# Rows of two units per batch by transposing DMAs in batches 4 to 7, and a new order of all steps, in an attention and routing kernel

## The chip, the cores and the metric

The kernel runs on one core of a Trainium2 chip. The metric is the device time of one execution in microseconds (us). The core's engines are TensorE (PE, its weight loads PEld), VectorE (DVE), ScalarE (ACT), GpSimd (POOL) and SyncE (SP); each runs its own list of instructions in order and waits on semaphores of the others.

## The reference

Eight batches of 448 tokens. First an attention without a softmax, for 12 heads of 64 columns:

```python
scores = scale * np.matmul(q, k.transpose(0, 1, 3, 2))
attn = np.maximum(scores, 0.0) ** 2 / S
x = np.matmul(attn, v)          # then (batch, token, 768)
```

Then in every batch the 128 tokens with the highest gate score get an expert's output added:

```python
scores = np.einsum('bsd,d->bs', x, w_gate)
top_idx = np.argpartition(-scores[b], capacity)[:capacity]
h = np.maximum(x[b, top_idx] @ w1, 0.0)        # 768 to 1024
ye = h @ w2                                     # 1024 to 768
out[b, top_idx] = x[b, top_idx] + g[:, None] * ye   # g = sigmoid(score); all other rows of out are x
```

## The kernel before

A batch is three units of four heads, so units 0 to 23 are the attention, unit u belonging to batch u // 3. The whole program is one list of steps, the text `ORDER`, written by a planner and emitted item by item: an engine runs its own instructions in the order in which they stand there. Moving an item in the list therefore changes what stands in front of it on its engine, and nothing else. Letters A and D in an item say whether ACT or DVE does the copy out of PSUM.

A unit goes through these steps (u the unit, c one of seven chunks of tokens):

- `L,q,u`, `L,k,u`, `L,v,u`: POOL issues the load of q, k or v (fp32 in DRAM, bf16 in SBUF; six buffers of each). For the units in `BYDMA` the heads are laid out in another way, and the load is issued as two halves of 64 partitions (line 115 and not line 111).
- `T` and `TE`: PE turns q and k, DVE copies them to `qkt`.
- `S,u,c`: PE makes the scores of a chunk (line 260) in two of the eight PSUM banks; `R,u,c`: ACT takes the ReLU of them into `r_sb` (line 216). There are 168 of these ReLUs. A later `S` that uses the same banks waits for the ReLU that empties them.
- `Q,u,c0,c1`: DVE squares `r_sb` into `a_sb`, in two pieces per unit; `V,u,c`: PE multiplies with v (line 281, 28 matmuls per unit).
- `X,u`: ACT or DVE copies the unit's output, token columns along the free axis, to `xT_sb`.
- The rows of the output, token by token, are made in one of two ways. `RT,u` has PE turn `xT_sb` back into PSUM (line 295) and `RE,u` copies it to `x_rows`; or `XB,u` has SP issue two transposing DMAs (line 320) from `xT_sb` to `x_rows`. Before, `XB` is used for all units of batches 5 and 6.
- `ST,b`: POOL issues the store of batch b's rows to `out` (two DMAs).

Each batch b is then routed: `colx`, `colE`, `bt`, `rk`, `cs`, `rank`, `hots`, `sel`, `sE` find the 128 token numbers `idx`; `XG,b` is an indirect gather on POOL (line 443) that reads the rows back from `out`, and so waits for `idx` and for the landing of `ST,b`; `XT` turns them on PE and `xeE` copies them; `gs` and `sig` give the gate; `h,b,f` are the first expert matmuls (line 483, eight steps), `hE` their ReLU into `hT`; `y,b,f` the second ones (line 499), `yE` the copy with the gate into `gye`; `ADD,b` is an indirect accumulating DMA on POOL into `out` (line 517). Batch 7 is not gathered: `xe,7` picks its rows from `x_rows` by matmuls (line 435), with `g,7` (line 353) for its scores, and its `ADD` goes in two halves.

So POOL's queue holds, in one order, the loads, stores, gathers and additions: what stands behind a store that waits for its rows is issued after it.

Of the kernel before, what the change touches and what calls it, by code (L numbers as in the profile page):

```python
# [21 lines left out]
def kernel(  # L22
# [314 lines left out]
    class Moe:  # L337
# [11 lines left out]

        def g(self, i, bank=None):  # L350
            if i == 0:
                self.at["g"] = bank
            nc.tensor.matmul(out=PS[:, self.at["g"], :S],
                             lhsT=wg_col[:, 1, i:i + 1].to_broadcast([128, 128]), rhs=self.xT[:, i].rearrange("p c n -> p (c n)")[:, :S],
                             start=(i == 0), stop=(i == NM - 1), skip_group_check=True)
# [189 lines left out]
    Q,5,0,3 cs0,0,4 cs,0,0 cs,0,1 V,4,0,6 L,v,7 cs,0,2 R,6,0,A V,4,1 V,4,2 S,6,1,0 V,4,3 V,4,4 S,6,2,2 V,4,5
    V,4,6 rank,0 hots,0 Q,5,3,7 R,6,1,A R,6,2,A T,8,0,4 ST,0 T,8,1 TE,8,2,D V,5,0,0 S,6,3,2 V,5,1 X,4,A S,6,4,6
    Q,6,0,3 V,5,2 V,5,3 V,5,4 V,5,5 R,6,3,A S,6,5,2 R,6,4,A R,6,5,A S,6,6,4 V,5,6 RT,4,0,6 R,6,6,A sel,0,7 sE,0
    T,9,0,2 L,k,9 T,9,1 X,5,A RE,4,D S,7,0,4 S,7,1,6 R,7,0,A Q,6,3,7 R,7,1,A colx,1,0,0 colx,1,1 colx,1,2
    S,8,0,4 RT,5,0,1 colE,1 S,7,2,6 bt,1,0 R,8,0,A W,0,4,6 TE,9,2,D S,8,1,2 S,8,2,4 RE,5,D rk,1,0 rk,1,2 L,k,10
    R,7,2,A W,1,6,8 L,q,10 RT,3,0,1 rk,1,1 W,0,2,6 S,7,3,6 R,8,1,A RE,3,D rk,1,3 R,8,2,A Q,7,0,3 V,6,0,2 V,6,1  # L550
    V,6,2 W,0,3,6 L,k,11 R,7,3,A V,6,3 V,6,4 S,7,4,4 R,7,4,A S,7,5,0 T,10,0,6 T,10,1 XG,0 S,7,6,4 TE,10,2,D
    V,6,5 R,7,5,A R,7,6,A V,6,6 X,6,A cs0,1,0 cs,1,0 cs,1,1 cs,1,2 rank,1 hots,1 W,1,2,8 XT,0,0,1 S,8,3,4
    S,8,4,6 R,8,3,A R,8,4,A xeE,0,2,D sel,1,0 sE,1 S,8,5,2 W,0,1,6 h,0,0,0 h,0,1 h,0,2 R,8,5,A S,8,6,4 S,9,0,6
    h,0,3 h,0,4 Q,7,3,7 h,0,5 S,9,1,2 h,0,6 Q,8,0,3 h,0,7 R,8,6,A S,9,2,4 R,9,0,A Q,8,3,7 V,7,0,6 V,7,1 L,v,8
# [10 lines left out]
    L,q,13 T,13,0,0 L,k,13 T,13,1 RE,8,D S,12,3,6 R,11,6,A RE,7,D V,10,0,4 V,10,1 V,10,2 L,q,15 V,10,3 TE,13,2,D
    L,v,12 L,k,17 L,v,14 S,12,4,2 V,10,4 V,10,5 R,12,3,A R,12,4,A S,12,5,0 Q,11,3,7 S,12,6,6 R,12,5,A R,12,6,A
    V,10,6 X,10,A hots,2 T,14,0,2 L,v,15 T,14,1 TE,14,2,D y,1,0,2,0 y,1,1,2 y,1,2,2 Q,12,3,7 L,k,15 S,13,0,6
    S,13,1,2 S,13,2,4 R,13,0,A L,v,13 R,13,1,A L,q,17 y,1,3,2 y,1,4,2 y,1,5,2 sel,2,6 L,k,19 R,13,2,A ST,2
    y,1,6,2 y,1,7,2 sE,2 S,13,3,2 V,11,0,6 R,13,3,A V,11,1 V,11,2 L,q,18 S,13,4,4 V,11,3 V,11,4 R,13,4,A
# [5 lines left out]
    TE,16,2,D cs,3,0 cs,3,1 cs,3,2 rank,3 XG,2 RE,10,A XT,2,0,1 xeE,2,2,D R,14,6,A Q,14,3,7 S,15,0,4 R,15,0,A
    S,15,1,6 S,15,2,2 R,15,1,A h,2,0,0 h,2,1 Q,14,0,3 h,2,2 R,15,2,A h,2,3 L,v,18 S,15,3,4 R,15,3,A S,15,4,6
    h,2,4 h,2,5 h,2,6 h,2,7 hE,2,2,D S,15,5,2 L,q,20 hots,3 V,14,0,4 V,14,1 L,v,17 R,15,4,A V,14,2 S,15,6,6
    L,k,22 V,14,3 V,14,4 V,14,5 V,14,6 Q,15,0,3 R,15,5,A R,15,6,A X,14,A L,q,21 S,16,0,0 S,16,1,2 R,16,0,A ST,3
# [92 lines left out]
```

## Time and profile before

| what | us |
|---|---|
| median of 3 runs | 200.74 (198.83 to 202.49) |
| the profiled execution | 199.68 |
| its span, first to last instruction | 197.9 |
| PE, DVE, ACT, POOL busy in the span | 179.1, 164.7, 162.5, 109.2 |
| mean granted share of PE's clock | 0.987 |

The profiled execution took 1.78 us more than its span, and 1.06 us less than the median. A matmul's busy time includes its passage through the array, so a busy PE may still be one that takes in little. The span has four parts: a start until the first ReLU, a long stretch in which ACT, DVE and PE all work nearly without a pause, a last stretch after the last ReLU in which PE works off the experts of batches 5 to 7, and the last additions.

### The profile page before, as it was taken

To read this page: it belongs to the slowest core of one execution; us is meant where nothing else is said; L and a number is where in the kernel's file an instruction comes from. 1 tells how busy PE (TensorE), PEld (TensorE's weight loads), DVE (VectorE), ACT (ScalarE), POOL (GpSimd) and SP (SyncE) were. 2 spreads that over 40 slices of the span, in tenths; PEclk is the share of its full clock that TensorE was granted. 3 is DMA by queue.
4 is the path that set the end of the run, shared out by engine and by line. 5 is a ranking of instruction groups with operands and counts; after the bars stand their busy time and mean duration, and the time that the engine had idled before them with its cause. 6 is when DMAs were issued, how large, how long until landed. Compare 5 with 4: busy or idle time off the path is not lost.

```text
span 197.9 us, 7244 instructions
## 1 busy us (share of the span) xinstructions
PE 179.1 (91%) x3186; PEld 124.1 (63%) x3186; DVE 164.7 (83%) x234; ACT 162.5 (82%) x204; POOL 109.2 (55%) x160
## 2 busy tenths in 40 slices
PE   7778898989899999999998999999999999999900
PEld 7455455657567675875776767776676466688600
DVE  2489999999989999999999899999997999753310
ACT  4689999999999998999998999899998997242300
POOL 7968654641863967758897694460203140853360
PEclk9999999999999999999999999999999999999995
...
GB/s 175 140 184 203 203 205 205 235 322 206 201 248 298 203 182 200 202 195 283 177 152 172 344 205 288 262 145 170 226 106 106 92 311 55 18 251 240 55 135 24
DMA packets 32333, 37.70 MB, mean 191 GB/s; under 512 B 8744, under 2 KB 29614, under 8 KB 31278
## 3 DMA queue, kind: packets, MB, share of 16 engines
...
## 4 chain that ended last, share of the span: by engine, by line
PE 56%; ACT 17%; DMA 11%; POOL 7%; issue 4%; DVE 2%; POOLq 0%; DVEq 0%
ACT r_sb L216 15%; PE ps L260 12%; PE ps L483 10%; PE ps L499 9%; PE ps L281 7%; PE ps L233 5%; DMA q_sb<-in_q_dram 4%; DMA v_sb<-in_v_dram 4%; PE ps L295 4%; POOL out_dram L517 3%; DMA xg<-out_dram,idx 3%; PE ps L209 2%; PE ps L374 2%; PE ps L362 2%; POOL k_sb L111 1%
## 5 line engine op out<-in xcount | busy, mean ns | idle before, releaser
L216 ACT ACTIVATE r_sb<-ps 128x896 bf16<-128x896 f32 x168 | 140.8, 955 | 8.1 <-PE ps L260 7.1
L274 DVE TENSOR_TENSOR a_sb<-r_sb 128x2688 bf16<-128x2688 bf16 (+1 forms) x48 | 84.9, 1785 | 2.4 <-ACT r_sb L216 2.0
L260 PE MATMUL ps<-qkt 64*64 64x448 bf16 x672 | 55.6, 362 | 4.3 <-ACT r_sb L216 2.5
L281 PE MATMUL ps<-a_sb,v_sb 64*64 64x448 bf16 x672 | 42.1, 351 | 0.8 <-ACT r_sb L216 0.8
L260 PEld LDWEIGHTS <-qkt 64*64 64x64 bf16 x672 | 21.4, 104 | 21.7 <-issue 11.4
L220 DVE COPY qkt<-ps 128x1792 bf16<-128x1792 bf16 (+3 forms) x26 | 26.1, 1006 | 4.4 <-PE ps L233 2.8
L281 PEld LDWEIGHTS <-v_sb 64*64 64x64 bf16 x672 | 21.5, 106 | 9.5 <-issue 2.2
L443 POOL DMA_INDIRECT xg<-out_dram,idx x7 | 12.2, 1748 | 27.4 <-DVE idx L427 23.6
L499 PE MATMUL ps<-w_sb,hT 128*128 128x384 bf16 x128 | 25.2, 326 | 0.0
L483 PE MATMUL ps<-xeT,w_sb 128*128 128x128 bf16 x384 | 24.5, 219 | 0.2 <-DVE xeT L220 0.2
L483 PEld LDWEIGHTS <-w_sb 128*128 128x128 bf16 x384 | 21.8, 98 | 4.5 <-issue 4.2
L517 POOL DMA_INDIRECT out_dram<-gye,idx x9 | 15.7, 1741 | 9.5 <-ACT g__3725 L476 5.9
L216 ACT ACTIVATE xT_sb<-ps 128x896 bf16<-128x896 f32 x16 | 15.4, 963 | 3.0 <-PE ps L281 2.9
L111 POOL DMA_DIRECT2D v_sb<-in_v_dram x18 | 13.2, 731 | 6.5 <-PE ps L281 2.8
L327 POOL DMA_DIRECT2D out_dram<-x_rows x8 | 4.5, 567 | 21.9 <-DMA x_rows<-xT_sb 13.6
L233 PEld LDWEIGHTS <-q_sb 128*64 128x64 bf16 x336 | 11.2, 111 | 6.5 <-issue 5.5
L233 PE MATMUL ps<-ident,q_sb 128*64 128x128 bf16 x336 | 14.1, 223 | 1.1 <-ACT r_sb L216 0.6
L499 PEld LDWEIGHTS <-hT 128*128 128x128 bf16 x128 | 10.6, 97 | 7.2 <-issue 2.2
L111 POOL DMA_DIRECT2D q_sb<-in_q_dram x17 | 12.7, 749 | 4.0 <-PE ps L233 1.5
L111 POOL DMA_DIRECT2D k_sb<-in_k_dram x17 | 12.5, 736 | 3.5 <-PE ps L260 1.5
L233 PE MATMUL ps<-ident,k_sb 128*64 128x128 bf16 x336 | 13.9, 220 | 0.0
L385 DVE SCALAR_TENSOR_TENSOR mask_sb<-ps,cols,tie 128x448 bf16<-128x448 f32 (+2 forms) x24 | 12.3, 546 | 0.7 <-PE ps L374 0.6
(123 smaller groups left out, 196.7 us busy)
## 6 DMA issues: line engine op xcount, KB each, us to landing
...
```

Of the source, the lines that this page charges most:

```text
L111: nc.gpsimd.dma_start(out=dst, in_=src(t, u))
L216: nc.scalar.activation(out=out_, in_=in_, func=func or AF.Copy, scale=scale)
L220: nc.vector.tensor_copy(out=out_, in_=in_)
L233: nc.tensor.matmul(out=PSB[HALF[j], at["T", u, w], n * 128:(n + 1) * 128], lhsT=s[:, j, c, :], rhs=ident, is_transpose=True, start=(n == 0 ...
L260: nc.tensor.matmul(out=PS[HALF[hf], bank + j, :S], lhsT=qkt[u][HALF[j], 1, c, hf, :], rhs=qkt[u][HALF[j], 0, :, hf, :], start=True, stop=True)
L274: nc.vector.tensor_tensor(out=a_sb[u][:, c0:c1], in0=r, in1=r, op=ALU.mult)
L281: nc.tensor.matmul(out=PS[HALF[j], at["V", u] + hf, :S], lhsT=v_sb[u % NBUF][HALF[hf], j, c, :], rhs=a_sb[u][HALF[hf], c, j, :], start=(c ...
L385: nc.vector.scalar_tensor_tensor(out=mask, in0=row[:, o:S], scalar=self.cols[:, c:c + 1], in1=tie[:, :S - o], op0=ALU.subtract, op1=ALU.is ...
L443: read = reads[self.b] = nc.gpsimd.indirect_dma_start(out=self.xg, out_offset=None, in_=out[0:self.b + 1].rearrange("b s d -> (b s) d"), i ...
L483: nc.tensor.matmul(out=PS[:, self.at["h"] + bk, o:o + 128], lhsT=w1_sb[:, m, f * 128:(f + 1) * 128], rhs=self.xeT[:, m, :], start=(m == 0) ...
L499: nc.tensor.matmul(out=PS[:, self.at["y"] + w, :384], lhsT=self.hT[:, f, :], rhs=w2_sb[:, f, w * 384:(w + 1) * 384], start=(f == 0), stop= ...
L517: add = nc.gpsimd.indirect_dma_start(out=out[0:self.b + 1].rearrange("b s (w d) -> (b s w) d", w=w), out_offset=bass.IndirectOffsetOnAxis( ...
```

## The change

`BYDMA` now holds units and not batches: the first two units of each of the batches 4, 5, 6 and 7 (12, 13, 15, 16, 18, 19, 21 and 22) take the transposing DMAs, eight units in place of six; the third unit of each of these batches goes over PE. The gate's column for such a unit is looked up unit by unit (`order`). `h` and `y` get an argument `by64` that splits a matmul's 128 output rows into two halves of 64; it is 0 for all of `h` and 1 for eight steps of `y`, `y,1,4` to `y,1,7` and `y,2,4` to `y,2,7`. The list `ORDER` is a new one throughout: its planner now charges transfers for later loads that overtake them.

```diff
-    BYDMA = (5,6)
+    BYDMA = (12,13,15,16,18,19,21,22)
...
-        if b not in BYDMA:
+        if u not in BYDMA:
             nc.gpsimd.dma_start(out=dst, in_=src(t, u))
             return
...
+        def order(self, m):
+            return 1 - (NU * self.b + m // 2 in BYDMA)
...
-                                     rhs=wg_col[:, 1 - (self.b in BYDMA), m:m + 1],
+                                     rhs=wg_col[:, self.order(m), m:m + 1],
...
-        def y(self, f, part, bank=None):
+        def y(self, f, part, by64, bank=None):
...
-                nc.tensor.matmul(out=PS[:, self.at["y"] + w, :384], lhsT=self.hT[:, f, :],
-                                 rhs=w2_sb[:, f, w * 384:(w + 1) * 384], start=(f == 0),
-                                 stop=(f == NF - 1), skip_group_check=True)
+                for p in HALF if by64 else (slice(0, 128),):
+                    nc.tensor.matmul(out=PS[p, self.at["y"] + w, :384], lhsT=self.hT[:, f, p],
+                                     rhs=w2_sb[:, f, w * 384:(w + 1) * 384], start=(f == 0),
+                                     stop=(f == NF - 1), skip_group_check=True)
...
-    hE,5,2,D V,22,0,4 V,22,1 V,22,2 V,22,3 V,22,4 V,22,5 V,22,6 R,23,5,A R,23,6,A sel,6,0 y,5,0,2,6 y,5,1,2
+    V,22,0,4 V,22,1 V,22,2 V,22,3 V,22,4 V,22,5 V,22,6 R,23,4,A R,23,5,A S,23,6,0 R,23,6,A y,5,0,2,0,2 y,5,1,2,0
```

On ACT, at the end of the attention, there stood (`r_sb_3457` and `r_sb_3589` are the ReLUs of units 22 and 23, `xT_sb1` batch 7's output, `g` a gate):

```order
L476 ACTIVATE g__2525<-ps_84 128x1
L216 ACTIVATE r_sb_3457<-ps_84 128x896 x6
L216 ACTIVATE r_sb_3589<-ps_84 128x896 x7
L216 ACTIVATE xT_sb1_104<-ps_84 128x2x448 x2
L476 ACTIVATE g__2994<-ps_84 128x1
```

And now (`r_sb_3424` and `r_sb_3626` are units 22 and 23, `gye_3612` belongs to batch 4, `hT_3673` to batch 5):

```order
L216 ACTIVATE r_sb_3424<-ps_84 128x896 x6
L216 ACTIVATE gye_3612<-ps_84,g__2541 128x768
L216 ACTIVATE r_sb_3626<-ps_84 128x896 x3
L216 ACTIVATE hT_3673<-ps_84 128x1024
L216 ACTIVATE r_sb_3626<-ps_84 128x896 x4
L216 ACTIVATE xT_sb1_104<-ps_84 128x2x448 x2
```

Two copies that DVE did before, batch 4's `gye` and batch 5's `hT`, now stand between ACT's last ReLUs.

On POOL, in the last third of the program, there stood (`v_sb5` takes unit 23's values, `v_sb4` unit 22's, `x_rows_3076` and `x_rows_3439` are batches 5 and 6, `xg` a gather, `gye` an addition):

```order
L443 DMA xg_3087<-out_0_dram,idx_2524 128x768
L111 DMA v_sb5_102<-in_v_dram 128x2x448
L327 DMA out_0_dram<-x_rows_3076 64x3072
L328 DMA out_0_dram<-x_rows_3076 64x2304
L443 DMA xg_3451<-out_0_dram,idx_2993 128x768
L111 DMA v_sb4_101<-in_v_dram 128x2x448
L327 DMA out_0_dram<-x_rows_3439 64x3072
L328 DMA out_0_dram<-x_rows_3439 64x2304
L517 DMA out_0_dram<-gye_3115,idx_2130 1792x768
```

And now (`x_rows_3283` is batch 6, `v_sb3` and `v_sb5` take the values of units 21 and 23, `gye_2103` and `gye_3169` belong to batches 1 and 3):

```order
L446 DMA xg_3428<-out_0_dram,idx_3019 128x768
L335 MEMSET gap_116 1x1
L523 DMA out_0_dram<-gye_2103,idx_1078 896x768
L115 DMA v_sb3_100<-in_v_dram 64x2x448 x2
L327 DMA out_0_dram<-x_rows_3283 64x3072
L328 DMA out_0_dram<-x_rows_3283 64x2304
L523 DMA out_0_dram<-gye_3169,idx_2189 1792x768
L111 DMA v_sb5_102<-in_v_dram 128x2x448
L446 DMA xg_3773<-out_0_dram,idx_3502 128x768
```

The values of unit 23, the last load of all, moved from in front of batch 5's store to behind batch 6's store and batch 3's addition.

On DVE, at the end of the attention, there stood (`a_sb` are the squares of units 22 and 23, `idx_3384` batch 6's token numbers, `x_rows_3765` the rows of units 22 and 21):

```order
L222 TENSOR_SCALAR xT_sb1_104<-ps_84 128x2x448
L409 TENSOR_TENSOR hot__3383<-slots_127,rank__3382 128x512
L218 TENSOR_SCALAR hT_3676<-ps_84 128x1024
L274 TENSOR_TENSOR a_sb_3716<-r_sb_3589 128x2688
L427 TENSOR_REDUCE idx_3384<-ps_84 128x1
L274 TENSOR_TENSOR a_sb_3716<-r_sb_3589 128x3584
L220 COPY x_rows_3765<-ps_84 128x4x256 x2
L368 TENSOR_TENSOR cols_3720<-ps_84,skew_106 128x4
```

And now:

```order
L430 TENSOR_REDUCE idx_3502<-ps_84 128x1
L274 TENSOR_TENSOR a_sb_3635<-r_sb_3424 128x2688
L222 TENSOR_SCALAR xT_sb1_104<-ps_84 128x2x448
L274 TENSOR_TENSOR a_sb_3786<-r_sb_3626 128x2688
L274 TENSOR_TENSOR a_sb_3786<-r_sb_3626 128x3584
L371 TENSOR_TENSOR cols_3763<-ps_84,skew_106 128x4
```

Batch 6's token numbers moved ahead of unit 22's second square, and the two copies of rows behind the last square are gone.

## Rows read from the trace of the kernel before

**Rows 1.** Busy time by stretch: us, then PE, PEld, DVE, ACT, POOL busy (instructions)

```profile
7.20:160.90 153.70, 146.29 (x2714) 99.20 (x2710) 144.58 (x196) 147.62 (x184) 89.63 (x128) 1.00 1.12 209
160.90:167.90 7.00, 7.00 (x130) 4.93 (x130) 6.75 (x6) 5.87 (x8) 0.00 (x0) 1.00 0.57 129
167.90:188.30 20.40, 20.34 (x285) 15.32 (x283) 9.97 (x26) 6.34 (x10) 10.48 (x12) 1.00 0.67 139
188.30:197.90 9.60, 0.00 (x0) 0.00 (x0) 0.59 (x1) 0.00 (x0) 2.95 (x3) 0.74 0.52 77
```

**Rows 2.** ACT's waits: us in total, times, the longest

```profile
ACT r_sb L216 <- PE ps L260: 7.1, 15, 1.1
```

**Rows 3.** Groups by form: busy us, mean ns of one, idle before

```profile
L216 ACT ACTIVATE r_sb<-ps 128x896 bf16<-128x896 f32 x168 | 140.8, 955 | 8.1 <-PE ps L260 7.1 <-ACT g__604 L476 0.5
...
L216 ACT ACTIVATE xT_sb<-ps 128x896 bf16<-128x896 f32 x16 | 15.4, 963 | 3.0 <-PE ps L281 2.9
...
L222 DVE TENSOR_SCALAR xT_sb<-ps 128x896 bf16<-128x896 f32 x8 | 8.7, 1089 | 0.4 <-ACT r_sb L216 0.2
...
L295 PE MATMUL ps<-ident,xT_sb 128*64 128x128 bf16 x32 | 1.2, 220 | 0.0
```

**Rows 4.** The same view: the copies that change engine

```profile
L220 DVE COPY x_rows<-ps 128x1024 bf16<-128x1024 bf16 x16 | 10.9, 685 | 1.1 <-PE ps L295 1.0
...
L216 ACT ACTIVATE x_rows<-ps 128x1024 bf16<-128x1024 bf16 x2 | 2.0, 1024 | 0.4 <-DMA xg<-out_dram,idx 0.3
...
L216 ACT ACTIVATE hT<-ps 128x1024 bf16<-128x1024 f32 x1 | 1.0, 1024 | 3.2 <-PE ps L397 3.2
...
L216 ACT ACTIVATE gye<-ps,g__3385 128x768 f32<-128x768 f32 x1 | 0.9, 902 | 4.9 <-issue 4.9
```

**Rows 5.** Timeline of the start: start, us, engine, what [idle before]

```profile
5.52 0.60 ACT L216 ACTIVATE qkt<-ps 128x512 bf16<-128x512 bf16 x1 [0.99 <-PE ps L233]
...
6.15 0.56 DVE L220 COPY qkt<-ps 128x384 bf16<-128x384 bf16 x2 [0.83 <-ACT qkt L216]
```

**Rows 6.** Timeline of PE after the last scores

```profile
165.74 0.57 PE L260 MATMUL ps<-qkt 64*64 64x448 bf16 x8
166.14 1.49 PE L281 MATMUL ps<-a_sb,v_sb 64*64 64x448 bf16 x28
167.57 0.29 PE L422 MATMUL ps<-tok,hot__3383 128*128 128x2 bf16 x4
167.72 1.14 PE L499 MATMUL ps<-w_sb,hT 128*128 128x384 bf16 x6
...
171.47 0.62 PE L295 MATMUL ps<-ident,xT_sb 128*128 128x128 bf16 x8
171.93 0.34 PE L362 MATMUL ps<-wg_col,xT_sb 128*128 128x1 bf16 x8
...
178.57 1.53 PE L435 MATMUL ps<-hot__3723,x_rows 128*128 128x128 bf16 x24
...
186.94 1.30 PE L499 MATMUL ps<-w_sb,hT 128*128 128x384 bf16 x7
```

**Rows 7.** The transposing DMAs: ns min, median, max of an issue; us to landing

```profile
L320 SPq DMA_TRANSPOSE x_rows<-xT_sb x12: 1189/1282/2214, 123.9 to 152.1; - x12
...
DMA to landing us min/median/max: 4.5/5.6/8.5
```

**Rows 8.** Timeline of POOL: unit 23's values, batch 6's store, batch 3's addition

```profile
131.79 0.73 POOL L111 DMA_DIRECT2D v_sb<-in_v_dram  x1 [0.54 <-PE ps L260]
...
157.47 0.57 POOL L327 DMA_DIRECT2D out_dram<-x_rows  x1 [6.54 <-DMA x_rows<-xT_sb]
...
158.87 1.68 POOL L517 DMA_INDIRECT out_dram<-gye,idx  x1 [0.30 <-issue]
```

**Rows 9.** The whole loads of line 111

```profile
DMA to landing us min/median/max: 6.0/7.9/8.9
```

**Rows 10.** Timeline of ACT: the 148th ReLU

```profile
147.38 1.03 ACT L216 ACTIVATE r_sb<-ps 128x896 bf16<-128x896 f32 x1
```

More of the change, by code (lines that the diff above doesn't have):

```diff
@@ L353, in g @@
             nc.tensor.matmul(out=PS[:, self.at["g"], :S],
[L354 removed]
+                             lhsT=wg_col[:, self.order(i), i:i + 1].to_broadcast([128, 128]), rhs=self.xT[:, i].rearrange("p c n -> p (c n)")[:, :S],
                              start=(i == 0), stop=(i == NM - 1), skip_group_check=True)
@@ L482, in h @@
             for m in range(NM):
-                nc.tensor.matmul(out=PS[:, self.at["h"] + bk, o:o + 128],
-                                 lhsT=w1_sb[:, m, f * 128:(f + 1) * 128], rhs=self.xeT[:, m, :],
-                                 start=(m == 0), stop=(m == NM - 1), skip_group_check=True)
+                for p in HALF if by64 else (slice(0, 128),):
+                    nc.tensor.matmul(out=PS[p, self.at["h"] + bk, o:o + 128],
+                                     lhsT=w1_sb[:, m, f * 128 + p.start:f * 128 + p.stop],
+                                     rhs=self.xeT[:, m, :], start=(m == 0), stop=(m == NM - 1),
+                                     skip_group_check=True)
         def hE(self, part, eng):
@@ L545 @@
[L545 to L554, printed above, removed]
@@ L565 @@
[L565 to L569, printed above, removed]
@@ L575 @@
[L575 to L578, printed above, removed]
-    T,17,0,6 T,17,1 colx,4,0,4 TE,17,2,D RT,14,0,5 sel,3,0 sE,3 colx,4,1 colx,4,2 R,16,1,A S,16,2,6 R,16,2,A
@@ new lines @@
+    V,7,3 L,k,13 V,7,4 V,7,5 V,7,6 Q,9,0,3 T,11,0,0 S,9,5,6 T,11,1 TE,11,2,D S,9,6,2 X,7,A R,9,5,A R,9,6,A
+    V,8,0,4 V,8,1 V,8,2 L,k,12 S,10,0,6 R,10,0,A V,8,3 V,8,4 V,8,5 S,10,1,2 Q,9,3,7 L,v,9 ST,1 V,8,6 X,8,A
+    T,12,0,0 T,12,1 L,k,16 W,1,6,8 S,10,2,6 colx,2,0,4 colx,2,1 R,10,1,A R,10,2,A TE,12,2,D gs,0,5 colx,2,2
+    RT,6,0,2 colE,2 sel,1,3 sE,1 RE,6,D sig,0 S,11,0,6 S,11,1,0 R,11,0,A RT,7,0,3 RE,7,D bt,2,2 S,10,3,4
+    S,10,4,6 R,11,1,A rk,2,1 R,10,3,A RT,8,0,3 rk,2,0 V,9,0,0 rk,2,3 V,9,1 R,10,4,A RE,8,D S,11,2,4 R,11,2,A
@@ new lines @@
+    h,1,4,0 h,1,5,0 R,12,3,A R,12,4,A L,k,15 h,1,6,0 h,1,7,0 S,12,5,0 S,12,6,4 R,12,5,A L,v,10 R,12,6,A ST,2
+    V,10,0,6 V,10,1 V,10,2 V,10,3 V,10,4 V,10,5 L,q,18 Q,11,3,7 S,13,0,0 V,10,6 hE,1,2,D R,13,0,A S,13,1,2
+    R,13,1,A T,14,0,4 T,14,1 S,13,2,0 R,13,2,A X,10,D V,11,0,6 V,11,1 V,11,2 TE,14,2,D S,13,3,2 V,11,3 V,11,4
+    V,11,5 L,q,15 V,11,6 R,13,3,A X,11,A Q,12,3,7 S,13,4,0 L,k,19 sel,2,4 sE,2 gs,1,5 sig,1 y,1,0,2,0,2
+    y,1,1,2,0 R,13,4,A y,1,2,2,0 Q,12,0,3 y,1,3,2,0 Q,13,0,3 S,13,5,4 R,13,5,A S,14,0,6 S,14,1,0 y,1,4,2,1
@@ new lines @@
+    S,16,6,4 bt,4,6 RT,14,0,7 y,2,0,2,0,0 Q,15,3,7 XB,12 y,2,1,2,0 R,16,5,A R,16,6,A sel,3,2 sE,3 gs,2,3
+    y,2,2,2,0 L,q,22 sig,2 y,2,3,2,0 S,17,0,2 RE,14,A L,v,16 R,17,0,A S,17,1,4 Q,16,0,3 R,17,1,A y,2,4,2,1
+    y,2,5,2,1 y,2,6,2,1 y,2,7,2,1 rk,4,3 yE,2,2,A T,18,0,2 rk,4,0 rk,4,1 L,v,18 rk,4,2 T,18,1 TE,18,2,D S,17,2,4
+    R,17,2,A V,15,0,6 V,15,1 V,15,2 S,17,3,0 V,15,3 V,15,4 V,15,5 R,17,3,A V,15,6 X,15,A S,17,4,2 R,17,4,A XG,3
+    Q,16,3,7 T,19,0,4 T,19,1 TE,19,2,D cs0,4,0 cs,4,0 cs,4,1 cs,4,2 rank,4 XT,3,0,1 L,q,21 L,v,20 xeE,3,2,D
@@ new lines @@
+    RE,20,D colx,6,0,5 colx,6,1 R,21,6,A colx,6,2 colE,6 S,22,2,2 Q,21,3,7 S,22,3,6 R,22,1,A S,22,4,0
+    y,4,0,2,0,4 R,22,2,A R,22,3,A R,22,4,A y,4,1,2,0 y,4,2,2,0 bt,6,2 rk,6,1 rk,6,3 y,4,3,2,0 XT,5,0,3 S,22,5,6
+    rk,6,0 S,22,6,0 R,22,5,A y,4,4,2,0 y,4,5,2,0 ADD,1 y,4,6,2,0 y,4,7,2,0 xeE,5,2,D cs0,6,3 L,v,21 h,5,0,0,6
+    h,5,1,0 ST,6 R,22,6,A cs,6,0 cs,6,1 yE,4,2,A rk,6,2 cs,6,2 rank,6 hots,6 S,23,0,0 S,23,1,4 R,23,0,A ADD,3
+    R,23,1,A S,23,2,2 R,23,2,A Q,22,3,7 h,5,2,0 h,5,3,0 h,5,4,0 h,5,5,0 h,5,6,0 h,5,7,0 hE,5,2,A L,v,23 sel,6,0
@@ new lines @@
+    h,6,4,0 h,6,5,0 rk,7,1 cs0,7,5 cs,7,0 cs,7,1 cs,7,2 h,6,6,0 h,6,7,0 RE,23,D rk,7,3 rank,7 hot,7,2 XB,22
+    y,5,7,2,0 ADD,2 xe,7,0,4 hot,7,1 xe,7,1 xe,7,2 ADD,4 hE,6,2,A y,6,0,2,0,0 hot,7,3 y,6,1,2,0 y,6,2,2,0 xe,7,3
+    xeE,7,1,D yE,5,2,A y,6,3,2,0 y,6,4,2,0 sig,6 y,6,5,2,0 y,6,6,2,0 xeE,7,0,D h,7,0,0,2 h,7,1,0 y,6,7,2,0
+    h,7,2,0 h,7,3,0 h,7,4,0 yE,6,2,A h,7,5,0 h,7,6,0 h,7,7,0 hE,7,1,A gs,7,0 sig,7 hE,7,0,D y,7,0,0,0,4
+    y,7,0,1,0 y,7,1,1,0 ST,7 y,7,2,1,0 y,7,3,1,0 y,7,4,1,0 y,7,5,1,0 y,7,6,1,0 y,7,7,1,0 ADD,5 sel,7,0 yE,7,1,A
```

128 lines of the change are left out of this document (63 added, 65 removed).

## The prediction

> **What bounds the kernel now.** I read the busy time by stretch first, then what ACT waits for, then the costs of the copies, and last the timelines of the two ends. From 7.20 us, when the first ReLU starts, to 160.90, when the last ReLU of unit 22 ends, ACT is busy 147.62 of 153.70 us, DVE 144.58 and PE 146.29 [rows 1]. The reader is to see that ACT and DVE both have almost nothing left there: ACT idles 6.1 us, DVE 9.1. PE's figure says less, since a matmul's time includes its passage. ACT is the first to bind: its 168 ReLUs alone take 140.8 us, 0.84 each [rows 3]. What it waits for is PE's scores, 7.1 us in 15 pieces, the longest 1.1 [rows 2]. So in this stretch an item of ACT costs its length, and an item of PE, POOL or a queue costs only what it makes ACT wait.
>
> From 160.90 to 167.90 come the last seven ReLUs (5.87 us busy and 1.13 idle); from 167.90 to 188.30 PE is busy 20.34 of 20.40 us while ACT and DVE are half idle or more: PE sets the end of that stretch. The last 9.6 us are the two additions of batch 7 and their landing [rows 1]. The profiled execution is 199.68 us, 1.06 below the median of the runs. I make the sum on the 199.68 and add the 1.06 at the end.
>
> **The start.** Before, ACT copied the first 512 columns of the turned q from 5.52 to 6.12, and DVE followed with 384 of q and 256 of k until 6.71, upon which the first scores started [rows 5]. Now DVE takes the 512 and the 384, and ACT the 256 of k beside it. DVE's two take about 0.4 + 0.36 us by its rate in these rows, an estimate, from about 5.5: done at 6.3. Gain 0.4; the ends are 0 (the warming matmuls that stand ahead of the scores end later) and 0.5.
>
> **The long stretch, to the end of unit 22's ReLUs.** ACT loses two `X` (2 x 0.96 = 1.93) to DVE and gains two `RE` (2 x 1.02 = 2.05): +0.1. DVE gains two `X` (2 x 1.09 = 2.18) and loses those two `RE` (2 x 0.685 = 1.37): +0.8, inside its 9.1 us of pauses [rows 1, 3, 4]. The number of turns by PE up to here is the same, 15 before and 15 now: batches 5 and 6 get two (units 17 and 20), batch 4 loses two, so no gain is to be had here from the transposing DMAs. The eight split steps of `y` double their matmuls. The nearest row is the turn of a unit, done 16 times in halves or 8 times whole: the 32 half-width ones of two units keep PE busy 1.2 us, 0.6 a unit, and a whole one takes 0.62 [rows 3, 6]. The halves cost nothing there, so I take 0 of a bound of 8 x 0.33 = 2.6 us, which would fall on PE and reach ACT in part only. Six more loads in halves cost POOL a second issue each, and POOL is idle for 64 of these 154 us. What stays open is ACT's idle time in a list that is new throughout. I keep it at 6.1 us; half of it and half as much again are the bounds, -3.1 and +3.1.
>
> So unit 22's last ReLU ends at 160.9 - 0.4 + 0.1 = 160.6.
>
> **From there to PE's last matmul.** ACT now has batch 4's `gye` (0.90) and batch 5's `hT` (1.02) among its last ReLUs [rows 4]. Alone that moves the last ReLU back by 1.9 us, less the 1.13 of idle time that stood there. But PE's work is what counts. The banks of unit 23's last scores are given free by the fifth ReLU of that unit, at 160.6 + 0.9 + 1.0 + 5 x 0.84 = 166.7; the scores take 0.36, so they end at 167.05. Before, they ended at 166.31 [rows 6].
>
> Before, PE worked on from 166.31 to 188.24, 21.9 us. Of that, three things go: unit 22's `V` (166.14 to 167.57, 1.43), which now stands ahead of the last scores, where PE waits for ACT anyway; batch 6's `sel` (167.57 to 167.72, 0.15), also earlier; and the turns of units 21 and 22, 0.46 each (171.47 to 171.93 for one of them), which the transposing DMAs take over [rows 6]. 21.9 - 1.43 - 0.15 - 0.92 = 19.4. One wait is added: unit 23's last square starts at the last ReLU's end, 168.4, and takes 2.0 on DVE; PE comes to it after six steps of `y` (0.97 for three, from 167.72), some small matmuls (about 0.5, an estimate) and three chunks of `V` (0.2 each), at 170.1, and waits 0.3. PE ends at 167.05 + 19.4 + 0.3 = 186.75, where it ended at 188.24: **1.5 us earlier**, the 0.3 of the parts before included.
>
> Two things could be late in it. The rows of unit 22 come from SP: the copy of its output follows ACT's last ReLU and ends at 169.35; the second transposing DMA is issued 1.28 later and lands 5.6 after that, at 176.2. PE needs it for `xe,7`, which begins 9.67 us ahead of PE's end [rows 6], at 177.1: 0.9 us to spare. With the longest issue and landing (2.21 and 8.5) it is 180.1, 3.0 late [rows 7]. And batch 5's `gye` and `hT` of batch 6 move to ACT, which is half idle there: 0.
>
> **The additions** keep their place behind the last copies: 9.6 us, 0. The sum is 199.68 - 1.5 = 198.2, and 199.2 at the level of the median.
>
> **The rivals.** *The new list also takes ACT's waits away.* The order was chosen with other charges for transfers, and half of the 7.1 us of waits [rows 2] may go: 199.2 - 3.6 = 195.6. For it speaks that ACT's waits are many and short, so that a better order could remove them; against it, that a transfer ends hardly any of them by the rows, and transfers are what the new charge is about.
>
> *The last values come too late.* Before, POOL issued unit 23's v at 131.79, 38 us ahead of its use [rows 8]. Now that load stands behind batch 6's store and batch 3's addition, and the store waits for the transposing DMAs of unit 19. By its place in the list unit 19's output is copied beside the 148th ReLU, which starts at 147.4 [rows 10], by DVE, done at 148.5; unit 18's copy stands one ReLU ahead, so SP starts on unit 18's two DMAs at about 147.4. With middle values the last one of unit 19 is issued at 151.2 and lands at 156.8 [rows 7]; the store is issued at about 157, as before, takes 1.1 with its second half, the addition 2.0 with its pause, the load goes out at 160.1 and lands 7.9 later, at 168.0 [rows 8, 9]. PE wants it at 169.55, after its six `y`. The margin is 1.5 us, and it is gone when the transposing DMAs land after 158.3. With the longest issue and landing they land at 162.5, the load at 173.5, and PE stands for 3.9 us: 203.1, slower than before. The rival beats the gain of 1.5 from a landing of about 159.9 on. (The Trainium skill, DMA: Bandwidth & Descriptors, "Anatomy of one DMA — SWDGE (gpsimd) path", gives about 2.0 us plus the bytes at 436 GB/s for a DMA from POOL; for this load's 459 KB read that is an estimate of 3.1 us, by which it would land at 168.7 even with the store at its latest, and this rival would not exist. The rows' 6.0 to 8.9 us, measured with other transfers queued, speak against using it here, and the sum goes by them.)
>
> *The rows of batch 7 come too late*, by the 3.0 us worked out above, since SP's DMAs now stand in the last stretch, where PE's turn had no such landing: 202.2. It decides when the second DMA of unit 22 takes more than 7.8 us from the copy's end. The trace has no transposing DMA beside the additions, so the middle value is as near as the rows come.
>
> **How the numbers follow.** The forecast of 199.2 has a chance of 0.45, with its own range of 197.2 to 201.2 for the small terms. The waits gone: 0.27. The last values late: 0.14. The rows late: 0.14. Measurement here tells changes of about 2%, 4 us: faster means under 196.7, slower over 204.8. Three quarters of the second case and a small part of the first are under 196.7: 0.27. Slower by that much needs one of the two late cases together with more idle time on ACT (+3.1): 0.11. The rest, 0.62, is no change. For 8 in 10 the range runs from the better half of the waits case, 195.4, to the worst landing, 203.4.
>
> **What would show it.** Right: the last ReLU at 168 to 169, PE's last matmul near 186.8, PE with no pause over 0.5 us from the last scores on, unit 23's v landing before its `V`, and ACT's idle time from 7 to 161 us near 6. Wrong: waits of ACT for scores far from 7 us in total, a pause of PE at `V` of unit 23 or at `xe` that a DMA ends, or split `y` steps that take twice as long. The weakest step is ACT's idle time, carried over from another list.

## The result, and the profile after

The changed kernel takes 197.43 us (median of 4 runs, 196.49 to 197.75), the kernel before on the same chip 200.01 (4 runs). The ratio is 0.986, with a 95% interval of 0.982 to 0.991: 1 to 2% faster, less than the 2% that the prediction took as the bound. The profiled execution took 197.75 us, its span 195.9. The forecast was 199.2, or 198.2 for the profiled execution.

The stretches, as in [rows 1], cut at the same events (the first ReLU, the ends of unit 22's and unit 23's last ReLUs, PE's last matmul); columns are start:end, us, then PE, PEld, DVE, ACT, POOL busy, PE's clock, DMA share, GB/s:

```profile
6.62:158.62 152.00, 144.76 (x2742) 98.99 (x2739) 143.71 (x193) 147.13 (x184) 94.78 (x133) 1.00 1.19 211
158.62:167.40 8.78, 8.78 (x155) 6.19 (x153) 6.71 (x7) 7.71 (x10) 4.10 (x5) 1.00 0.76 150
167.40:186.44 19.04, 18.23 (x257) 13.60 (x254) 7.35 (x20) 6.60 (x11) 5.92 (x8) 1.00 0.85 170
186.44:195.90 9.46, 0.00 (x0) 0.00 (x0) 0.00 (x0) 0.58 (x1) 3.01 (x3) 0.78 0.47 66
```

Unit 22's last ReLU ends at 158.62 and not at 160.90: 2.28 us earlier, where 0.3 was forecast. PE's last matmul ends at 186.44 and not at 188.24: 1.80 earlier. So the long stretch gave more than the whole, and the next one gave some back. ACT's waits, as in [rows 2], fell from 7.1 to 5.5 us:

```profile
ACT r_sb L216 <- PE ps L260: 5.5, 12, 0.9
```

On ACT the last ReLUs have batch 4's `gye` and batch 5's `hT` between them, and the very last ReLU waits 0.83 for its scores. The second fence has DVE's squares at that place, the first piece of unit 22's and the last of unit 23's:

```profile
158.52 0.90 ACT L216 ACTIVATE gye<-ps,g__2541 128x768 f32<-128x768 f32 x1
159.63 2.54 ACT L216 ACTIVATE r_sb<-ps 128x896 bf16<-128x896 f32 x3 [0.20 <-PE ps L260]
162.20 1.02 ACT L216 ACTIVATE hT<-ps 128x1024 bf16<-128x1024 f32 x1
163.12 2.53 ACT L216 ACTIVATE r_sb<-ps 128x896 bf16<-128x896 f32 x3
166.48 0.92 ACT L216 ACTIVATE r_sb<-ps 128x896 bf16<-128x896 f32 x1 [0.83 <-PE ps L260]
```

```profile
162.45 1.55 DVE L274 TENSOR_TENSOR a_sb<-r_sb 128x2688 bf16<-128x2688 bf16 x1
...
167.43 2.02 DVE L274 TENSOR_TENSOR a_sb<-r_sb 128x3584 bf16<-128x3584 bf16 x1 [0.65 <-ACT r_sb L216]
```

PE in the same place, as in [rows 6]. The reader is to see the order scores, V of unit 22 (from 164.15, right behind the scores ahead of it), last scores, `y`, V of unit 23, and the two pauses, one at V of unit 23 that the last square ends, one at `xe,7` (line 438) that a DMA ends:

```profile
163.93 0.36 PE L260 MATMUL ps<-qkt 64*64 64x448 bf16 x4
164.15 1.52 PE L281 MATMUL ps<-a_sb,v_sb 64*64 64x448 bf16 x28
165.47 0.39 PE L260 MATMUL ps<-qkt 64*64 64x448 bf16 x4
...
168.37 0.76 PE L281 MATMUL ps<-a_sb,v_sb 64*64 64x448 bf16 x12
169.51 0.95 PE L281 MATMUL ps<-a_sb,v_sb 64*64 64x448 bf16 x16 [0.38 <-DVE a_sb L274]
...
176.20 0.33 PE L438 MATMUL ps<-hot__3766,x_rows 128*128 128x128 bf16 x3
176.96 1.01 PE L438 MATMUL ps<-hot__3766,x_rows 128*128 128x128 bf16 x15 [0.43 <-DMA x_rows<-xT_sb]
```

The DMA is the transposing one of unit 22, the last one issued before that. Line 320 as in [rows 7], first SP's issues (ns min, median, max), then us to landing; below it POOL, where unit 23's values (line 111) stand behind the store and batch 3's addition, as against [rows 8]:

```profile
L320 SPq DMA_TRANSPOSE x_rows<-xT_sb x16: 1189/1366/2465, 105.5 to 170.4; - x16
...
DMA to landing us min/median/max: 3.9/7.6/10.4
```

```profile
154.78 0.55 POOL L327 DMA_DIRECT2D out_dram<-x_rows  x1 [1.91 <-DVE cols L371]
155.31 0.55 POOL L328 DMA_DIRECT2D out_dram<-x_rows  x1
156.16 1.64 POOL L523 DMA_INDIRECT out_dram<-gye,idx  x1 [0.30 <-issue]
157.24 1.37 POOL L111 DMA_DIRECT2D v_sb<-in_v_dram  x1
```

The load was issued at 157.24 and no row of PE's V of unit 23 waits for it (the 0.38 is DVE's).

### The profile page after: what moved, and what is told of

It reads as the page before. It is cut to its first block, busy times and chain, and to the rows that moved or that the text cites. A ratio compares the mean times of both kernels' runs of the same rounds, so it can differ in the third digit from the quotient of the medians.

```text
span 195.9 us, 7310 instructions
## 1 busy us (share of the span) xinstructions
PE 176.9 (90%) x3209; PEld 123.2 (63%) x3209; DVE 159.9 (82%) x228; ACT 164.5 (84%) x208; POOL 113.3 (58%) x166
## 4 chain that ended last, share of the span: by engine, by line
PE 53%; ACT 15%; DVE 12%; DMA 8%; issue 5%; POOL 2%; SPq 1%; DVEq 0%; POOLq 0%
PE ps L260 13%; ACT r_sb L216 13%; PE ps L281 10%; PE ps L487 8%; PE ps L505 8%; PE ps L233 7%; DVE a_sb L274 5%; DVE qkt L220 4%; DMA xg<-out_dram,idx 3%; DMA x_rows<-xT_sb 3%; PE ps L295 3%; DMA qf<-in_q_dram 2%; ACT xT_sb L216 2%; POOL out_dram L523 2%; DVE xT_sb L222 1%
## 5 line engine op out<-in xcount | busy, mean ns | idle before, releaser
L281 PE MATMUL ps<-a_sb,v_sb 64*64 64x448 bf16 x672 | 42.6, 351 | 0.9 <-ACT r_sb L216 0.5
L260 PEld LDWEIGHTS <-qkt 64*64 64x64 bf16 x672 | 21.9, 104 | 21.2 <-issue 10.2
L446 POOL DMA_INDIRECT xg<-out_dram,idx x7 | 13.2, 1880 | 26.2 <-DVE idx L430 15.1
L505 PE MATMUL ps<-w_sb,hT 128*128 128x384 bf16 (+1 forms) x144 | 24.8, 326 | 0.8 <-issue 0.7
L523 POOL DMA_INDIRECT out_dram<-gye,idx x9 | 16.5, 1837 | 5.9 <-ACT gye L216 4.0
L505 PEld LDWEIGHTS <-hT 128*128 128x128 bf16 (+1 forms) x144 | 11.3, 100 | 8.1 <-issue 3.1
L216 ACT ACTIVATE xT_sb<-ps 128x896 bf16<-128x896 f32 x14 | 13.6, 970 | 2.3 <-PE ps L281 2.3
L111 POOL DMA_DIRECT2D v_sb<-in_v_dram x16 | 12.4, 775 | 3.9 <-DMA k_sb<-in_k_dram 1.3
L111 POOL DMA_DIRECT2D k_sb<-in_k_dram x15 | 11.9, 790 | 4.5 <-issue 1.7
L115 POOL DMA_DIRECT2D k_sb<-in_k_dram x16 | 9.9, 639 | 5.0 <-DMA w_sb<-in_moe_w_dram 1.4
L111 POOL DMA_DIRECT2D q_sb<-in_q_dram x15 | 11.3, 756 | 2.6 <-PE ps L260 1.1
```

What stands on the lines that cost most here:

```text
L115: nc.gpsimd.dma_start(out=dst[HALF[g]], in_=t[b, h0:h0 + 2].rearrange("j (p c) d -> p j (c d)", c=NC))
L216: nc.scalar.activation(out=out_, in_=in_, func=func or AF.Copy, scale=scale)
L260: nc.tensor.matmul(out=PS[HALF[hf], bank + j, :S], lhsT=qkt[u][HALF[j], 1, c, hf, :], rhs=qkt[u][HALF[j], 0, :, hf, :], start=True, stop=True)
L281: nc.tensor.matmul(out=PS[HALF[j], at["V", u] + hf, :S], lhsT=v_sb[u % NBUF][HALF[hf], j, c, :], rhs=a_sb[u][HALF[hf], c, j, :], start=(c ...
L446: read = reads[self.b] = nc.gpsimd.indirect_dma_start(out=self.xg, out_offset=None, in_=out[0:self.b + 1].rearrange("b s d -> (b s) d"), i ...
L505: nc.tensor.matmul(out=PS[p, self.at["y"] + w, :384], lhsT=self.hT[:, f, p], rhs=w2_sb[:, f, w * 384:(w + 1) * 384], start=(f == 0), stop= ...
```

## The experiments

Twelve kernels ran. A ratio is to the kernel before on the same chip, as is the changed kernel's 0.986. For the long stretch I compare the time from the end of unit 1's first ReLU to the end of unit 22's last, where ACT's idle time is the length less its busy time; the rows stand together behind the third experiment.

**1. The new units in the old order.** `BYDMA` as now, `ORDER` as before, but `RT`/`RE` of units 12, 13, 21 and 22 replaced by `XB`, and `XB` of 17 and 20 by `RT`/`RE`.

```diff
-    BYDMA = (5,6)
+    BYDMA = (12,13,15,16,18,19,21,22)
...
-    R,14,5,A rk,3,0 RT,12,1,0 RE,12,D T,15,0,4
+    R,14,5,A rk,3,0 XB,12 T,15,0,4
```

> The order of before, with the new choice of units for the transposing DMAs alone (units 12, 13, 21, 22 go to them, 17 and 20 back to PE's turns). Theory, the gain is the new order's: ACT paces the long stretch and has the same work, so unit 22's last ReLU ends within 0.7 us of before's 160.9; in the last stretch two turns (0.92 us) go and a wait for the rows at xe of 0.4 to 3 us comes; ratio to before 0.995 to 1.010. Rival, the choice of units makes the gain: ratio near 0.986, with the last ReLU of unit 22 near 158.6.

Measured: 208.02 us, ratio 1.048 (1.040 to 1.056). Neither the theory (at most 1.010) nor the rival had that. The four runs lie far apart, from 204.48 (the profiled one) to 209.65 us, 2.8 to 5.4% above the median of the kernel before beside them (198.83). In the profile the stretch takes 150.72 us, and ACT idles 9.5 of them, 4.3 more than in the kernel before. The longest piece, 2.31, stands at batch 3's gather. First POOL's timeline, with columns as in [rows 8], then PE's, then ACT's:

```profile
115.35 0.62 POOL L115 DMA_DIRECT2D q_sb<-in_q_dram  x1 [0.93 <-DMA q_sb<-in_q_dram]
116.95 0.59 POOL L115 DMA_DIRECT2D q_sb<-in_q_dram  x1 [0.99 <-DMA out_dram<-x_rows]
118.96 1.54 POOL L446 DMA_INDIRECT xg<-out_dram,idx  x1 [1.41 <-DMA v_sb<-in_v_dram]
```

```profile
125.37 0.53 PE L295 MATMUL ps<-ident,xg 128*64 128x128 bf16 x12 [1.79 <-DMA xg<-out_dram,idx]
125.83 0.38 PE L260 MATMUL ps<-qkt 64*64 64x448 bf16 x4
```

```profile
126.26 3.46 ACT L216 ACTIVATE r_sb<-ps 128x896 bf16<-128x896 f32 x4 [2.31 <-PE ps L260]
```

POOL stands three times, for 3.3 us in all, twice at loads that come in halves and once at the gather itself; the gather goes out at 118.96, PE turns its rows 1.79 us late, the next scores stand behind that on PE, and ACT idles 2.31. So in the old order the choice of units makes the kernel 3 to 5% slower, and what makes the changed kernel faster must come with its list. The new list with the old choice of units was not tried.

**2. Only the tail's part of it, in the old order.** Batches 5 and 6 whole by DMA as before, and units 21 and 22 too.

```diff
-    BYDMA = (12,13,15,16,18,19,21,22)
+    BYDMA = (15,16,17,18,19,20,21,22)
```

> The kernel before, in its own order, with units 21 and 22 by transposing DMAs and all the rest as it was (batches 5 and 6 whole by DMA). With the eight new units in the old order the kernel took 4.8% more than before; of its eight units 12 and 13 are new in batch 4, 21 and 22 in batch 7. Theory: the loss came from batch 4, where gathers and loads wait in POOL's queue behind the store of rows; 21 and 22 alone cost nothing and give 0 to 0.9 us, ratio 0.995 to 1.002. Rival: the transposing DMAs at the end collide with batch 6's gather and the additions, or hold SP: 2 us or more slower, ratio over 1.01.

Measured: 200.31 us, ratio 1.007 (1.004 to 1.010), between the two numbers. The stretch is as before, so the loss of experiment 1 comes from batch 4's units and the two others that change, not from 21 and 22. In the profile PE ends, and the last addition is issued, within 0.1 us of the kernel before. The two turns are saved, but PE waits now at V of unit 23 and at batch 6's gather:

```profile
170.36 0.95 PE L281 MATMUL ps<-a_sb,v_sb 64*64 64x448 bf16 x16 [0.31 <-DVE a_sb L274]
174.43 0.51 PE L295 MATMUL ps<-ident,xg 128*128 128x128 bf16 x6 [0.51 <-DMA xg<-out_dram,idx]
```

0.82 of the 0.92 us that the turns took come back as waits. Where the 0.7% of the timed runs lies, the profile doesn't show.

**3. Who sets the pace of the long stretch.** Three kernels add work to the changed one, about 5 us each: idle matmuls of zeros on PE (`PW`), 16 of them in the banks of the next scores; first expert steps done twice, in banks that they hold anyway; and ReLUs done twice.

```diff
-    S,5,3,4
+    PW,16,4 S,5,3,4
```

> The changed kernel with idle matmuls added on PE in the long stretch: 16 matmuls of zeros ahead of the fourth scores of each of units 5, 8, 11, 14, 17 and 20, 0.88 us a piece, 5.3 us in all. They compute nothing that is used. Theory: ACT sets the pace of this stretch, with its ReLUs' lengths, and PE has time to spare between the scores: at most 2 of the 5.3 us reach the end, ratio 0.986 to 0.996. Rival: PE sets the pace and ACT's waits for scores are its shadow: all 5.3 us reach the end, ratio 1.013, and ACT's waits on line 260 grow by 5 us.

```diff
-    h,1,0,0,2 h,1,1,0
+    h,1,0,0,2 h,1,0,0,2 h,1,1,0 h,1,1,0
```

> The changed kernel with 16 first expert matmul steps done twice, the first four of each of the batches 1 to 4; they stand in the long stretch, use the banks that they hold anyway, and write the same result again. 6 matmuls a step, 0.335 us, 5.3 us of PE in all. This parts two readings of the run with 96 idle matmuls, which took 5.3 us of PE too and cost nearly all of it: those stood in the bank of the next scores, so that each also waited for a ReLU. Theory now: PE has no more time to spare in the long stretch than ACT has, and its work is paid nearly in full wherever it stands: unit 22's last ReLU ends at 162 to 164 where the changed kernel has 158.6, ratio 1.005 to 1.013. Rival (the prediction's view: ACT sets the pace, PE has room): at most 2 us, ratio 0.986 to 0.996.

```diff
-    R,5,3,A
+    R,5,3,A R,5,3,A
```

> The changed kernel with six ReLUs of the long stretch done twice (the fourth of units 5, 8, 11, 14, 17 and 20), 0.81 to 0.84 us each, 5.0 us of ACT in all; they write the same values again. Theory (the prediction's): ACT sets the pace and all of it reaches the end, ratio 1.010 to 1.012, unit 22's last ReLU at 163 to 164. Rival: PE alone sets the pace and ACT's waits for scores (5.5 us) take up most of it: at most 2.5 us, ratio under 0.999. Between the two, if ACT and PE hold each other up in turn: 3 to 4 us.

Measured: ratios 1.011 (1.006 to 1.017), 1.010 (1.007 to 1.012) and 1.015 (1.013 to 1.018), that is 2.4 to 2.9% above the changed kernel. The stretch (columns as in the first rows above) in the kernel before, the changed one, the one with idle matmuls, with doubled expert steps, with doubled ReLUs, and in experiment 1:

```profile
14.74:160.90 146.16, 140.29 (x2597) 94.94 (x2591) 139.22 (x183) 140.93 (x176) 83.59 (x119) 1.00 1.12 211
```

```profile
13.71:158.62 144.91, 138.85 (x2633) 94.82 (x2628) 138.79 (x180) 140.42 (x177) 88.08 (x123) 1.00 1.19 212
```

```profile
13.72:163.04 149.32, 144.33 (x2729) 99.59 (x2724) 138.80 (x180) 141.25 (x176) 85.22 (x123) 1.00 1.14 207
```

```profile
13.71:161.88 148.17, 143.49 (x2729) 99.68 (x2724) 138.69 (x180) 140.96 (x177) 84.88 (x122) 1.00 1.14 209
```

```profile
13.71:163.17 149.46, 139.74 (x2633) 95.51 (x2628) 139.19 (x180) 145.85 (x183) 84.71 (x123) 1.00 1.11 206
```

```profile
15.07:165.79 150.72, 142.16 (x2593) 94.97 (x2588) 139.87 (x183) 141.21 (x177) 85.83 (x125) 1.00 1.14 209
```

Six kernels share the changed one's stretch (it, the late values of experiment 5, and experiments 6 and 7); their stretches are 143.94 to 144.91 long, 144.4 in the mean, with 140.7 of ACT and 3.7 idle. Against that the doubled ReLUs add 5.1 to ACT and 5.1 to the length: paid in full, idle time unchanged (3.6). The doubled expert steps add 4.6 to PE's busy time and 3.8 to the length; the idle matmuls add 5.5 and 4.9. So ACT's work is paid in full, as the prediction had it, but the view that PE has room falls: of an extra us on PE, 0.8 to 0.9 come out as ACT's waits (7.2 and 8.1 us idle). Each of these is one profile against a base that varies by 1 us.

ACT alone does not set the pace either. This is the profile's own account of the changed kernel, the chain of work that ended last, as shares of the span by engine:

```profile
PE 53%; ACT 15%; DVE 12%; DMA 8%; issue 5%; POOL 2%; SPq 1%; DVEq 0%; POOLq 0%
```

In the kernel before PE has 56% of that chain and ACT 17%. ACT and PE hold each other up in turn. Whether DVE, busy for 139 of these 145 us, does so too was not tried.

**4. The split `y`.** All eight steps whole again.

```diff
-    y,1,4,2,1
+    y,1,4,2,0
```

> The changed kernel with the eight split steps of y made whole again. Theory, the halves run side by side and PE has slack there: no change, 197.4 +- 1, and a whole step in the trace as long as a split one (0.33 us from start to start). Rival, a half costs as much as a whole matmul: the split cost PE 2.6 us, and the kernel gets up to 2 us faster without it.

Measured: 196.52 us, ratio 0.987 (0.984 to 0.989), the changed kernel's. The split costs nothing that can be measured. The two kinds of step by form (busy us, mean ns of one), first the split ones of the changed kernel, then the whole ones of this run:

```profile
L505 PE MATMUL ps<-w_sb,hT 128*64 128x384 bf16 x32 | 3.0, 329 | 0.0
```

```profile
L505 PE MATMUL ps<-w_sb,hT 128*128 128x384 bf16 x128 | 24.8, 326 | 0.0
```

The 32 halves keep PE busy for 3.0 us; 16 whole matmuls come to 3.1 by the second row. By chance this profile has neither of the two pauses in the last stretch, since the last square and unit 22's rows are in time: from the last scores' end at 166.57 to PE's end at 185.97 it is 19.40 us.

```profile
166.18 0.39 PE L260 MATMUL ps<-qkt 64*64 64x448 bf16 x4
...
176.34 1.17 PE L438 MATMUL ps<-hot__3750,x_rows 128*128 128x128 bf16 x18
```

**5. The start and the last values.** The kernel before with the first some forty steps of the new list, above all the new split of the first copies; and the changed kernel with unit 23's values behind batch 6's gather.

```diff
-    Cq,1 Cq,0 T,0,0,0 TQE,0,4,A Ck,0,2,D TK,0,2 TQE,4,7,D LFk,2,7 TKE,0,2,D
+    Cq,0 Cq,1 Ck,0,2,D T,0,0,0 TQE,0,4,D TK,0,2 TKE,0,2,A TQE,4,7,D LFk,2,7
```

> The order of before with the first some forty steps as in the changed kernel (which engine copies the first turned q and k, where the small constants stand). Theory, ACT paces all that follows: the first ReLU starts 0.5 us earlier, and unit 22's last ReLU and the end do so too by 0.4 to 0.9 us: ratio 0.995 to 0.998. Rival, transfers or DVE pace the long stretch: the first ReLU is earlier, but by unit 22 nothing of it is left (0 +- 0.2 us).

```diff
-    ADD,3 L,v,23 ... XG,6
+    ADD,3 ... XG,6 L,v,23
```

> The changed kernel with unit 23's load of v issued behind the last gather instead of in front of it. In the changed kernel it lands at about 164.5 and is used at 168.4. Theory, PE sets the last stretch and a late last load stops it one to one: issued at about 165, landing at 171 to 173, so PE stands 2.5 to 4.5 us at V of unit 23, and the time grows by as much: 200 to 202. Rival, the wait is taken up by slack behind it: under 1 us.

Measured: 198.81 us, ratio 0.998 (0.994 to 1.002), and 198.06 us, ratio 0.996 (0.993 to 1.000). The start alone is too small for the timing; in its profile the first ReLU starts at 6.86 (7.20 before), unit 22's last ends at 160.32, 0.58 earlier, and PE at 187.40, 0.84 earlier, so in this pair a gain at the start is carried to the end. The late values cost about 1% against the changed kernel's 0.986, some 2 us, less than the 2.5 to 4.5 of the theory. In the profiled execution PE stood only 0.85 us for them; that execution took 196.64 us, less than each of the nine others (197.72 to 199.62), so the trace doesn't show where the 1% went. POOL's issue with its landing, then PE's V of unit 23:

```profile
164.23 0.80 POOL L111 DMA_DIRECT2D v_sb<-in_v_dram  x1
...
DMA to landing us min/median/max: 4.3/4.3/4.3
```

```profile
168.61 1.52 PE L281 MATMUL ps<-a_sb,v_sb 64*64 64x448 bf16 x28 [0.85 <-DMA v_sb<-in_v_dram]
```

The load took 4.3 us from its issue to its landing, less than the 6.0 to 8.9 of [rows 9]. The place from which a late load costs is where the prediction put it: ahead of V of unit 23.

**6. Units 21 and 22 by PE's turns in the new order.** The `XB` of both out, `RT` and `RE` back where the kernel before had them; the loads of these units are whole again, and batch 5's `gs` and `sig` stand later.

```diff
-    XB,21 ... XB,22
+    y,5,1,2,0 RT,21,0,7 ... RE,21,D ... V,23,6 RT,22,0,4 RE,22,D XT,6,0,7
```

> The changed kernel with units 21 and 22 by PE's turns again, where the kernel before has them (behind the second step of batch 5's y, and behind unit 23's V), and no transposing DMA in the last stretch. Theory: PE has the two turns to do again, 0.92 us as in the prediction, and loses the wait at xe,7 (0.77 us in the profile of the changed kernel, none in some of its variants): 0.2 to 0.9 us slower, PE ends at 186.6 to 187.3, ratio 0.987 to 0.991. Rival 1: the turns' copies fall on a free DVE and the DMAs' absence frees the gather of batch 6: no slower, ratio 0.986 or less. Rival 2: unit 22's copy stands ahead of batch 6's XT copy and delays the gate: 1.5 us or more slower.

Measured: 196.66 us, ratio 0.989 (0.987 to 0.991): not to be told from the changed kernel. From the last scores' end at 165.77 to PE's end at 186.51 it is 20.74 us, beside 20.58 in the changed kernel: PE does the two turns again, and does not wait at `xe,7`. So in these two profiles the transposing DMAs in the last stretch give 0.2 us on balance. Experiment 4's profile has 19.40 there, so with rows and squares in time it can be 1.3.

**7. Taking the two pauses away.** Two additions earlier on POOL, so that fewer bytes move beside unit 22's DMAs; the last scores ahead of the last three chunks of unit 22's V; and both.

```diff
-    ADD,1 ... XG,6 ... ADD,2 ... ADD,4
+    ADD,1 ADD,2 ... ADD,4 XG,6
```

> The changed kernel with two additions issued earlier on POOL: batch 2's right behind batch 1's, batch 4's ahead of batch 6's gather. Theory: the packets of unit 21's and 22's transposing DMAs took 5 us and more in the changed kernel because these two additions and the gather moved bytes beside them; with two of the three gone from 167 to 173 us the rows of unit 22 land before 176.2, xe,7 does not wait (0.77 us lost there in the changed kernel), and the kernel gains 0.4 to 0.8 us, ratio to the kernel before 0.982 to 0.984 where the changed one has 0.986. Rival 1: SP's own issues (2.3 us each) set the landing, whatever else runs: the pause at xe,7 stays, ratio 0.986. Rival 2: the additions now stand ahead of loads and of the gather on POOL and make them late: the gather of batch 6 lands later and its XT waits, up to 2 us slower, ratio 0.996.

```diff
-    V,22,0,4 V,22,1 V,22,2 V,22,3 V,22,4 V,22,5 V,22,6 R,23,4,A R,23,5,A S,23,6,0 R,23,6,A
+    R,23,4,A V,22,0,4 V,22,1 V,22,2 V,22,3 S,23,6,0 V,22,4 V,22,5 V,22,6 R,23,5,A R,23,6,A
```

> The changed kernel with unit 23's last scores ahead of the last three chunks of unit 22's V, where they stood behind all seven. Theory: in the changed kernel ACT stood 0.83 us before its last ReLU since PE did unit 22's V first, and unit 23's last square came 0.38 us too late for V,23,3. Both go: the last ReLU ends about 0.8 us earlier, the pause at V,23,3 is gone, and PE ends 0.4 us earlier; ratio about 0.984 against 0.986. Rival: the pause moves on to xe,7, which waits for the rows of unit 22 by DMA, as long as these land at 176.9: PE's end stays, ratio 0.986.

> Both moves in one kernel: two additions earlier on POOL and the last scores ahead of the end of unit 22's V. Theory: the two pauses of PE behind the last scores (0.38 at V,23,3 and 0.77 at xe,7) stand one behind the other, and only both edits take both: -0.8 to -1.1 us, ratio 0.981 to 0.982. Rival: another wait takes their place (the gather of batch 6, or the gate's sums ahead of xe,7), and the ratio is 0.985 or more.

Measured: 198.1 us, ratio 0.991 (0.987 to 0.994); 197.31, 0.989 (0.985 to 0.993); and 197.09, 0.985 (0.982 to 0.989). None differs from the changed kernel's 0.986 by more than the intervals. The profiles show why the single moves gain nothing. With the additions early, PE does not wait at `xe,7`, but it gets there at 176.95, when the rows had landed in the changed kernel too; it stands 1.03 us at batch 6's turned rows instead, whose gather now goes out at 165.72 (162.82 in the changed kernel). With the scores early, the pause at V of unit 23 is gone, and `xe,7` waits for 0.35 and 0.45 us. (The first row names ACT's gate as what ended the wait. In the changed kernel the same matmuls began at 170.39, ahead of that gate, which was computed from 171.32 on, so they don't need it; the line below, from the waits of the same matmuls' weight loads, names the gather.)

```profile
171.14 0.51 PE L295 MATMUL ps<-ident,xg 128*128 128x128 bf16 x6 [1.03 <-ACT g__3020 L479]
...
  DMA xg<-out_dram,idx: 1.5, 1
```

```profile
176.03 0.23 PE L438 MATMUL ps<-hot__3766,x_rows 128*128 128x128 bf16 x1 [0.35 <-DMA x_rows<-xT_sb]
176.71 1.01 PE L438 MATMUL ps<-hot__3766,x_rows 128*128 128x128 bf16 x15 [0.45 <-DMA x_rows<-xT_sb]
```

With both, PE has no pause from the last scores on, and the span is the shortest of all the profiled executions, 194.3 us. `xe,7` runs through; it has unit 22's rows by 175.4, where they came at 176.7 with the scores alone moved. That fits the theory that the additions slow unit 22's DMAs, but it is one pair of profiles:

```profile
175.21 1.17 PE L438 MATMUL ps<-hot__3768,x_rows 128*128 128x128 bf16 x18
```

Of the 1.6 us between the two spans, 0.4 lie ahead of unit 22's last ReLU, where the list is the same. What is left, about 1 us, is too little for these intervals: a version that surely beats the changed kernel was not found.

## Why the prediction held, step by step

**The sum.** 198.2 was forecast for the profiled execution and 197.75 measured; against the median 199.2 and 197.43, inside the forecast's own range of 197.2 to 201.2. The other part of the distance is the 1.06 that was added for the median: a fourth run of the kernel before brought that median down to 200.01, 0.33 above its profiled time. The sum is right because errors nearly cancel, which is luck: it put unit 22's last ReLU 1.98 us too late, then the last scores 0.79 and PE's work behind them 0.88 too early. One of the prediction's signs of being wrong came true, a pause of PE at `xe,7` that a DMA ends.

**The start** was forecast at 0.4. The first ReLU starts 0.58 earlier, and ACT's pause before unit 1's first ReLU shrank from 0.85 to 0.38, which the prediction did not see. Together unit 1's first ReLU ends 1.03 earlier in the profile, 0.8 in the mean of the six kernels against three with the old start (14.0 and 14.8). By the same means the first ReLU itself starts 0.3 earlier (6.93 and 7.22), so the forecast was near and the profiled pair is a favourable one.

**The long stretch.** Of the 2.28 us that unit 22's last ReLU is earlier, 1.03 are there at unit 1; 0.51 more come from ACT's work in this pair of profiles and 0.74 from its idle time. ACT's own work was forecast at +0.1 and is -0.1 by the mean of the six against the three with the old list outside experiment 1 (140.7 and 140.8). The halves of `y` at 0 were right (experiment 4). The step that failed is ACT's idle time, "I keep it at 6.1 us": over the same stretch, from the first ReLU on, it is 4.9. From unit 1 on the old list has 5.2, 5.1 and 5.6 us, the new one 3.1 to 4.5 in the six. So 0.7 us came from there in the pair and 1.6 in the mean. That is the first rival, the waits that go, at less than half of its 3.6. All six kernels have less idle time than the three with the old list, but experiment 4's, whose list is the new one but for the whole steps of `y`, has 4.9 us, close to the old 5.1: the size of the gain is not settled. Which of the list's many moves removed the waits was not tried.

**To the last scores** the prediction had 6.45 us after unit 22's last ReLU; it took 7.24. It let the banks' ReLU set the start of these scores. But they also stand behind all of unit 22's V on PE, and PE has no pause there: it is busy for 8.78 of the 8.78 us from 158.62 on. The fifth ReLU ends at 164.84, 6.2 after unit 22's last where 6.1 was forecast, and the scores start at 165.47 only, when PE has done that V. So the wait was for PE and not for a bank. The 0.83 us of ACT's pause follow from it, and experiment 7 removes them by moving the scores.

**PE's last stretch.** 19.4 us of work was forecast, and 19.40 is what PE takes where it does not wait (experiment 4). The wait at V of unit 23 was forecast at 0.3 and is 0.38. **The rows of unit 22** had 0.9 us to spare by the prediction, and came 0.6 too late: the 18 matmuls of `xe,7` took from 176.20 to 177.97, 1.77 us where they take 1.17 without a wait. The copy of its output was done at 168.21, the second DMA was issued 2.14 later and not 1.28, and by the profile's chain it landed after 6.56 and not 5.6. So the third rival came true at a fifth of its 3.0 us. The additions took 9.46 where 9.6 was said.

**The last values** were not late. SP issued unit 19's last DMA at 148.24 and not at 151.2, so the store went out at 154.78 and not at 157, the load at 157.24 and not at 160.1. Experiment 5 shows the rival's mechanism, a load 7 us later, at 0.85 us in the profile; the timing has 1%. On the estimate from the Trainium skill (DMA: Bandwidth & Descriptors, "Anatomy of one DMA — SWDGE (gpsimd) path"), by which this load would take 3.1 us: experiment 5 has it at 4.3 from issue to landing, and experiment 4, where it stands as in the changed kernel, at 6.4, so it can be well under the 6.0 to 8.9 of [rows 9], but not as short as the page's figure gives.
